# Windowed attention and a gated MLP on one core: value products of 128 and 64 keys, one pool of PSUM banks, and a new order of work

## Chip, cores, metric

The kernel runs on one core of a Trainium2 chip. The metric is the device time of one execution in microseconds, the median of several runs. Five engines work side by side, each through its own instructions in program order, and wait for each other by semaphores: TensorE (PE in the profile; PEld is its weight load), VectorE (DVE), ScalarE (ACT), GpSimd (POOL) and SyncE (SP), which here only issues DMA transfers.

## What is computed

```python
# q, k, v: (8 batches, 8 heads, 576 positions, 64)
scores = q @ k^T / 8                              # within each head
scores = where(0 <= t - s < 128, scores - slope[h] * (t - s), -1e9)
attn = softmax(scores)                            # with + 1e-9 under the sum
x = (attn @ v)  as (8, 576, 512)                  # heads side by side
h = gelu_tanh(x @ w_in)                           # w_in 512 x 1024
u, g = h[..., :512], h[..., 512:]
g = layer_norm(g) * g_ln
g = w_sg @ g + b_sg[:, None]                      # 576 x 576, mixes positions
out = x + (u * g) @ w_out
```

A query looks back at 127 positions and itself, so of each row of scores only 128 keys count.

## The kernel before

The work is cut into 32 pairs of heads (8 batches times 4 pairs) and, per batch, one MLP. Positions are cut into blocks of 64 (R = 64): block 0 comes first by itself, the other eight (numbers 1 to 8) go in four tiles of 128 (T = 4). A query block of 64 sees keys of three blocks, its own and the two before, and 64 of each 192 keys are out of its window in every row. The kernel folds: where a key of the query's own block lies in the future, the score of the key 128 positions earlier takes its place, so each query keeps exactly 128 scores.

A pair passes through these steps, each a letter in the list of work (with the pair's number behind it):

- `q`, `L`: DMA loads of queries and keys (one transfer) and of the values (six: two large ones into `vt`, two small ones, and two of 16 KB into a block-diagonal tile `vd`).
- `*` (or `a` and `c` for the first five pairs): scores, line L247, products of 64 rows by 64 columns, which run on the four quarters of the array.
- `A B C G`: fold (L273) and shift by the bias with a minimum per row (L266), on DVE. `e E f F j`: exponentials on ACT (L282). `R`: inverse of the sums on DVE. `r s S`: scaling on POOL (L299).
- `t T z`: transposes on TensorE (L309, L322). `X Y`: masks (L318), which split each transposed tile into the part that belongs to the own block and the part from 128 earlier, both 128 x 512, each a product of the PSUM tile with a mask (`m_old`, `m_own`). `P`: copy of the first block's weights.
- `2` or `3`: the values of the first block (L329), a product over the block-diagonal `vd`. `v` or `V`: the values of the other blocks (L342). For each head, each 128-key tile is multiplied with the masked weights of up to two query blocks: 6 products of 128 columns and 3 of 64 per head.
- `x`: gather of the two results from PSUM (L350, L351) on ACT. `h l k`: split into a high and a low part for the MLP's products.

The MLP's products run in three terms each (high x high, high x low, low x high, lines L559 to L561). Its steps are `v` (the half that is normalised; for batch 0 it is spread over `w` steps), `u`, `t` (the last 64 positions), then `y` (the mix over positions) and `O` (output). Their evacuations are `vg`, `uc`, `tj`, `gm` (L712) and `oa` (L742). `D` stores. At the start the two weight matrices, which arrive as 8-byte floats, are split into high and low parts: `i` loads, `d` starts on ACT, `m b o` on DVE (L183, L185, L187), `+` on POOL (L190), `H` on ACT, `-` on DVE or POOL (L194). `wl wH w-` do the same for the 4-byte mixing matrix.

The order of all this is one long list, `ORDER`, written out in the kernel. A planner walks it: it holds each step's engine, the steps it comes after and the buffers it takes, asserts that the list respects them, and emits the instructions; each engine then runs its instructions in the list's order. So a step that waits holds up everything behind it on its engine.

PSUM has eight banks of 512 columns. Before, they are three pools with two tiles each: `ps_s` and `ps_a` of one bank for the attention, `ps_m` of two banks for the MLP. One `ps_m` tile holds two steps, for instance `v10` and `v11`, or the two halves `y100` and `y101`, and is given back after the evacuation of both.

Of the kernel before, what the change touches and what calls it, by code (L numbers as in the profile page):

```python
# [21 lines left out]
def attention_gmlp(  # L22
# [30 lines left out]
    TINY64 = 2.0 ** -15  # L53
# [16 lines left out]
    def hi_of(x):  # L70
        return x[:, 0:S]
# [99 lines left out]
    def split64(hi, lo, w, f, last):  # L171
# [9 lines left out]
        nc.scalar.activation(f, w1f, AF.Abs)  # L181
        yield
        nc.vector.tensor_scalar(f, f, TINY64, None, ALU.max)  # L183
# [3 lines left out]
        nc.vector.scalar_tensor_tensor(out=fi, in0=w1, scalar=-0x40000000, in1=fi, op0=ALU.bitwise_and, op1=ALU.bitwise_or)  # L187
# [20 lines left out]
    class Pair:  # L208


        def __init__(self, n):
            self.n, self.b, self.hp = n, n // NPAIR, n % NPAIR
            self.vd, self.p0 = vds[n % 3], p0s[n % 3]
# [9 lines left out]
        def load_v(self):  # L223

            b, c0 = self.b, self.hp * 2 * D
            vt = self.vt = att.tile([P, 2 * T + 1, 2 * D], F32, name="vt", bufs=2)
            cs = slice(c0, c0 + 2 * D)
            for i in range(2):
                nc.sync.dma_start(vt[:, i * T:(i + 1) * T, :], v[b, i * R:i * R + T * P, cs].rearrange("(t p) d -> p t d", p=P))
                nc.sync.dma_start(vt[i * R:(i + 1) * R, 2 * T, :], v[b, 0:R, cs])  # L230
            for j, js in enumerate(self.heads):
                nc.sync.dma_start(self.vd[js, js], v[b, 0:R, c0 + j * D:c0 + (j + 1) * D])

        def scores(self, *t2s):
            insts = [x for t2 in t2s for x in self.score_list(t2, ps_a if len(t2s) > 1 and t2 == 0 else ps_s)]
            burst(insts)

        def score_list(self, t2, pool):
# [5 lines left out]
            banks = self.banks[t2] = [pool.tile([P, 512], F32, name=pool.name) for _ in range(2)]  # L244
# [23 lines left out]
        def minima(self, t2, j):  # L268
# [23 lines left out]
        def inverse(self):  # L292
            rr = self.rr = att.tile([P, NS], F32, name="rr", bufs=3)
# [13 lines left out]
        def transpose(self, j):  # L307
            ct = self.ct[j] = ps_a.tile([P, 512], F32, name="ps_a")
            burst([lambda t=t: nc.tensor.transpose(ct[:, t * P:(t + 1) * P], self.pr[j][:, t, :], ident) for t in range(T)])  # L309

        def masked(self, j):
# [3 lines left out]
            xv = x.rearrange("p (h t b c) -> p t h b c", h=2, t=T, b=2)  # L315
            cv = self.ct.pop(j).rearrange("p (t h c) -> p t h c", t=T, h=2)
            for i, m in enumerate((m_old, m_own)):
                nc.vector.tensor_tensor(xv[:, :, :, i, :], cv, m.rearrange("p (t h c) -> p t h c", t=1, h=1).broadcast_to([P, T, 2, R]), ALU.mult)  # L318
# [557 lines left out]
```

## Time and profile before

| | |
|---|---|
| median of 3 runs | 635.64 us (635.51 to 636.70) |
| the profiled execution | 635.48 us, span 633.8 us |
| busy share of the span | PE 95%, PEld 87%, DVE 59%, ACT 56%, POOL 37% |
| granted TensorE clock, mean | 0.985 of full |
| instructions | 14834, of them 5664 matrix products |
| DMA | 57.24 MB, mean 90 GB/s; 211 to 236 GB/s in the first tenth |
| largest groups on TensorE | the nine groups of the MLP's 288-column products, 2304 products, 75 to 79 us each |

A group's busy time is the sum of its instructions' durations. Products on TensorE are pipelined, so a product of 288 columns that lasts 295 ns is followed by the next 133 ns later; lengths in the chain that ended last tell more of their cost than their durations. Idle time of an engine is put down to what ended it.

### The profile page before, as it was taken

The numbers are of one execution on the slowest core, as the hardware profiler recorded it, in microseconds if no ns is written. First come the engines' busy times: TensorE is split into PE (matmuls) and PEld (weight loads), VectorE is DVE, ScalarE is ACT, GpSimd is POOL, SyncE is SP. The second block draws the span as 40 slices with busy tenths as digits, with TensorE's granted clock in tenths as the row PEclk, the third lists the DMA queues.
The fourth block names the chain that finished last, engine by engine and source line by source line (L and its number), as shares of the span: only waits on it lengthen the run. The fifth ranks groups of instructions, "written<-read, shape, count | busy, mean of one in ns | idle before, by whom it ended". The sixth has DMA issues, their size and how long they took to land.

```text
span 633.8 us, 14834 instructions
## 1 busy us (share of the span) xinstructions
PE 603.6 (95%) x5664; PEld 550.9 (87%) x5664; DVE 374.3 (59%) x1297; ACT 355.4 (56%) x1047; POOL 232.7 (37%) x237
## 2 busy tenths in 40 slices
PE   2687999989999999999999999999999999999997
PEld 1466799978999989998899989998999989999896
DVE  4779897537654786455723577647564565462611
ACT  6687768462673854834672578647473455543430
POOL 2668635542135222542134333542235221441220
PEclk9878999999999999999999999999999999999999
DMA  5777503241203243131220432333122311110001
GB/s 211 223 229 236 158 31 116 79 143 38 73 18 97 95 140 93 42 112 41 78 79 2 134 133 78 86 108 97 40 95 79 128 65 41 41 40 38 0 1 76
DMA packets 55931, 57.24 MB, mean 90 GB/s; under 512 B 8498, under 2 KB 45362, under 8 KB 55860
## 3 DMA queue, kind: packets, MB, share of 16 engines
q1 hardware_dynamic: 55860, 56.28, 28.5%
q8 instruction: 45, 0.74, 0.5%
q14 instruction: 26, 0.21, 0.1%
HBM read 46.83 MB, written 9.44 MB: 89 GB/s over the span
## 4 chain that ended last, share of the span: by engine, by line
PE 85%; DVE 4%; ACT 2%; issue 1%; POOL 0%; POOLq 0%; DVEq 0%
PE ps_m L559 21%; PE ps_m L561 20%; PE ps_m L560 20%; PE ps_s L342 8%; PE ps_a L309 4%; PE ps_a L247 4%; PE ps_s L247 3%; ACT e L282 1%; PE ps_m L707 1%; PE ps_m L706 1%; PE ps_m L643 1%; PE ps_m L645 1%; PE ps_s L329 1%; DVE px L318 1%; DVE e L266 1%
## 5 line engine op out<-in xcount | busy, mean ns | idle before, releaser
L282 ACT ACTIVATE e<-e,stats 128x128 f32<-128x128 f32 (+1 forms) x320 | 121.2, 381 | 39.4 <-DVE stats L266 38.4
L299 POOL TENSOR_TENSOR e<-e,rr 128x512 f32<-128x512 f32 (+1 forms) x96 | 80.1, 854 | 134.6 <-DVE rr L295 99.0
L559 PE MATMUL ps_m<-g,wo 128*128 128x288 f32 x256 | 78.7, 308 | 0.0
L559 PE MATMUL ps_m<-ws,vn 128*128 128x288 f32 x256 | 78.6, 307 | 0.0
L559 PE MATMUL ps_m<-xs,wi 128*128 128x288 f32 x256 | 77.6, 303 | 0.1
L561 PE MATMUL ps_m<-g,wo 128*128 128x288 f32 x256 | 75.8, 296 | 0.0
L561 PE MATMUL ps_m<-xs,wi 128*128 128x288 f32 x256 | 75.6, 295 | 0.0
L560 PE MATMUL ps_m<-ws,vn 128*128 128x288 f32 x256 | 75.6, 295 | 0.0
L561 PE MATMUL ps_m<-ws,vn 128*128 128x288 f32 x256 | 75.5, 295 | 0.0
L560 PE MATMUL ps_m<-xs,wi 128*128 128x288 f32 x256 | 75.5, 295 | 0.0
L560 PE MATMUL ps_m<-g,wo 128*128 128x288 f32 x256 | 74.9, 293 | 0.5 <-POOL g L719 0.5
L584 POOL TENSOR_TENSOR rs<-rs,mhalf 128x1 f32<-128x1 f32 (+1 forms) x40 | 31.4, 786 | 109.5 <-DVE rs L581 103.7
L359 POOL TENSOR_TENSOR xs<-xf,xs 128x576 fp32r<-128x576 f32 x32 | 45.4, 1425 | 62.0 <-ACT xs L356 62.0
L318 DVE TENSOR_TENSOR px<-ps_a,m_old 128x512 f32<-128x512 f32 x64 | 43.9, 686 | 41.1 <-PE ps_a L309 27.3
L719 POOL TENSOR_TENSOR g<-u,g 128x576 fp32r<-128x576 f32 x32 | 45.5, 1424 | 51.0 <-ACT g L716 51.0
L282 ACT ACTIVATION_READ_ACCUMULATOR e<-e,stats 128x1 f32 (+1 forms) x320 | 60.3, 188 | 0.0
L247 PE MATMUL ps_s<-qk 64*64 64x192 f32 (+2 forms) x632 | 42.2, 354 | 14.1 <-DMA qk<-qkT 7.9
L559 PE MATMUL ps_m<-wi,xs 128*128 128x512 f32 x128 | 53.6, 419 | 2.1 <-ACT vg L633 2.1
L712 DVE TENSOR_TENSOR u<-ps_m,u 128x576 f32<-128x576 f32 x32 | 24.1, 755 | 52.0 <-PE ps_m L707 49.8
L742 DVE TENSOR_TENSOR xf<-ps_m,xf 128x576 f32<-128x576 f32 x32 | 24.0, 752 | 49.3 <-PE ps_m L561 49.3
L560 PE MATMUL ps_m<-wi,xs 128*128 128x512 f32 x128 | 51.3, 401 | 0.0
L559 PEld LDWEIGHTS ps_m<-xs,wi 128*128 128x128 f32 x256 | 48.3, 188 | 3.4 <-issue 1.6
(122 smaller groups left out, 1523.4 us busy)
## 6 DMA issues: line engine op xcount, KB each, us to landing
qk<-qkT SPq DMA_DIRECT2D x32, 576.0 KB, 3.9
vt<-v_in SPq DMA_DIRECT2D x64, 256.0 KB, 3.5
outT<-xf SPq DMA_DIRECT2D x32, 288.0 KB, 2.1
wst<-w_in SPq DMA_DIRECT2D x8, 512.0 KB, 6.1
vt<-v_in SPq DMA_DIRECT2D x64, 32.0 KB, 3.1
wst<-w_out SPq DMA_DIRECT2D x4, 512.0 KB, 3.9
wst<-w_sgT SPq DMA_DIRECT2D x4, 288.0 KB, 5.1
vd<-v_in SPq DMA_DIRECT2D x64, 16.0 KB, 2.7
```

The source lines that it names most:

```text
L247: return lambda: nc.tensor.matmul(dst, qk[js, 0, q0:q0 + R], qk[js, 1, k0:k1], start=True, stop=True)
L282: nc.scalar.activation(x, x, AF.Exp, bias=self.nm[0:n, i:i + 1], scale=-1.0, accum_out=self.sm[0:n, i:i + 1])
L299: nc.gpsimd.tensor_tensor(x, x, self.rr[0:n, i:i + m].rearrange("p (m o) -> p m o", o=1).broadcast_to([n, m, c]), ALU.mult)
L309: burst([lambda t=t: nc.tensor.transpose(ct[:, t * P:(t + 1) * P], self.pr[j][:, t, :], ident) for t in range(T)])
L318: nc.vector.tensor_tensor(xv[:, :, :, i, :], cv, m.rearrange("p (t h c) -> p t h c", t=1, h=1).broadcast_to([P, T, 2, R]), ALU.mult)
L342: return lambda: nc.tensor.matmul(x1[heads[j], q0 + lo // 2 * R if t < 0 else q0 + t * R:q0 + (hi + 1) // 2 * R], block, px[j][:, (half * ...
L359: nc.gpsimd.tensor_tensor(lo_of(self.xs), self.xf, hi_of(self.xs).bitcast(F32), ALU.subtract)
L559: nc.tensor.matmul(dst, ah, bh, start=(first and i == 0), stop=False)
L560: nc.tensor.matmul(dst, ah, bl, start=False, stop=False)
L561: nc.tensor.matmul(dst, al, bh, start=False, stop=(last and i == n - 1))
L584: nc.gpsimd.tensor_tensor(x["rs"][0:rows], x["rs"][0:rows], mhalf[0:rows], ALU.pow)
L719: nc.gpsimd.tensor_tensor(st[f"g{f}"][:, 1, :], st["u"][:, f, :], st[f"g{f}"][:, 0, :].bitcast(F32), ALU.subtract)
```

## The change

- **Values.** `L` loads the values into ten slots of 128 keys (`vt[P, 2T + 2, 2D]`): one transfer of 256 KB to the lower 64 partitions, six of 64 KB, so that each query block finds its own keys and the block before it in one slot, with the own block in the upper or the lower half by the parity of the tile. The values step becomes 16 products over 128 keys with 64 columns (a query block against its own and the previous block), 14 over 64 keys (the fold, the block two before), and two over 64 keys for the first block, all in one burst `V`. The block-diagonal `vd` and the steps `2`, `3` are gone. The result lies in two banks, even tiles in one and odd tiles in the other, and `x` gathers it in four copies in place of two.
- **Masks.** `m_own` covers all of it; the second masked part is the tile minus the first part. The score fold (`minima`) mirrors this: the replaced block alternates with the tile's parity.
- **PSUM.** Eight single banks, handed out by the planner: a step takes the bank that is free earliest in the list. `u`, `y` and `O` take one bank per half (`uc`, `gm`, `oa` are done per half, too), `v` one per step.
- **Weights.** The split of the 8-byte floats loses one DVE step (`m`, L183), by a scale in the ACT step.
- **A new list.** It begins `q0 i0 i1 wl2 q1 a0 A0 c0 a1 c1 d0 b0 o0 e0 ...`; before it began `i0 q0 wl2 q1 i1 i7 d0 m0 b0 o0 +0 a0 A0 B0 c0 wl0 d7 d1 wH2 e0 ...`.

The diff, cut to its core:

```diff
-    ps_s = ctx.enter_context(tc.tile_pool(name="ps_s", bufs=2, space=PSUM))
-    ps_a = ctx.enter_context(tc.tile_pool(name="ps_a", bufs=2, space=PSUM))
-    ps_m = ctx.enter_context(tc.tile_pool(name="ps_m", bufs=2, space=PSUM))
+    ps = ctx.enter_context(tc.tile_pool(name="ps", bufs=1, space=PSUM))
+    psum = [ps.tile([P, 512], F32, name=f"bank{i}") for i in range(NB)]
+    def bank():
+        return psum[given.pop(0)]
...
-        nc.scalar.activation(f, w1f, AF.Abs)
+        nc.scalar.activation(f, w1f, AF.Abs, scale=REBASE)
         yield
-        nc.vector.tensor_scalar(f, f, TINY64, None, ALU.max)
+        nc.vector.tensor_scalar(fi, fi, 3, None, ALU.logical_shift_left)
         yield
-        nc.vector.tensor_scalar(fi, fi, 3, 0x3FFFFFFF, ALU.logical_shift_left, ALU.bitwise_and)
-        yield
...
-            for i in range(2):
-                nc.sync.dma_start(vt[:, i * T:(i + 1) * T, :], v[b, i * R:i * R + T * P, cs].rearrange("(t p) d -> p t d", p=P))
-                nc.sync.dma_start(vt[i * R:(i + 1) * R, 2 * T, :], v[b, 0:R, cs])
-            for j, js in enumerate(self.heads):
-                nc.sync.dma_start(self.vd[js, js], v[b, 0:R, c0 + j * D:c0 + (j + 1) * D])
+            nc.sync.dma_start(vt[0:R, 0:2 * T, :], blocks[:, 0:2 * T, :])
+            for slot, k in ((0, 1), (1, 2), (2, 0), (3, 2)):
+                nc.sync.dma_start(vt[R:P, slot:slot + 5:4, :], blocks[:, k:k + 5:4, :])
+            for rs, k in ((slice(0, R), 4), (slice(R, P), 3)):
+                nc.sync.dma_start(vt[rs, 2 * T:2 * T + 2, :], blocks[:, k:k + 5:4, :])
...
-            for i, m in enumerate((m_old, m_own)):
-                nc.vector.tensor_tensor(xv[:, :, :, i, :], cv, m.rearrange(...).broadcast_to([P, T, 2, R]), ALU.mult)
+            nc.vector.tensor_tensor(xv[:, 0], cv, over(m_own, 2), ALU.mult)
+            nc.vector.tensor_tensor(xv[:, 1], cv, xv[:, 0], ALU.subtract)
...
-        def values_first(self, pool):
-            self.x2 = pool.tile([P, 512], F32, name=pool.name)
-            nc.tensor.matmul(self.x2[:, 0:R], self.vd, self.p0, start=True, stop=True)
...
+            x1 = self.x1 = [bank() for _ in range(2)]
+            def dst(q):
+                t, half = divmod(q - 1, 2)
+                c0 = (t // 2 * 2 + half) * R
+                return x1[t % 2][:, c0:c0 + R]
+            def pair(q, j):
+                return lambda: nc.tensor.matmul(dst(q)[heads[j]], vt[:, PAIR_SLOT[q], heads[j]], px[j][:, (q - 1) * R:q * R], start=(q in (1, 3)), stop=False, skip_group_check=True)
+            def old(q, j):
+                rs = slice(0, R) if (q - 1) // 2 % 2 else slice(R, P)
+                return lambda: nc.tensor.matmul(dst(q)[heads[j]], vt[rs, OLD_SLOT[q], heads[j]], px[j][rs, (2 * T + q - 1) * R:(2 * T + q) * R], start=False, stop=False, skip_group_check=True)
+            def first(j):
+                return lambda: nc.tensor.matmul(x1[1 - j][heads[j], 2 * T * R // 2:2 * T * R // 2 + R], vt[heads[j], 2 * j, heads[j]], self.p0[heads[j]], start=False, stop=True, skip_group_check=True)
+            insts = [pair(q, j) for a, b in ((1, 3), (2, 4), (5, 7), (6, 8)) for q in (a, b) for j in range(2)]
+            insts += [old(3, 0), old(2, 0), old(3, 1), old(2, 1), old(4, 0), old(5, 0), old(4, 1), old(5, 1)]
+            insts += [old(7, 0), old(6, 0), old(7, 1), old(6, 1), old(8, 0), first(1), old(8, 1), first(0)]
...
-            nc.scalar.copy(xf[:, R:S].rearrange(...), self.x1.rearrange(...))
-            nc.scalar.copy(xf[:, 0:R], self.x2[:, 0:R])
+            for i, x in enumerate(self.x1):
+                nc.scalar.copy(xf[:, R:S].rearrange("p (a t c) -> p a t c", t=2, c=2 * R)[:, :, i, :], x[:, 0:T * R].rearrange("p (a c) -> p a c", a=2))
+                hs = self.heads[1 - i]
+                nc.scalar.copy(xf[hs, 0:R], x[hs, T * R:T * R + R])
...
+                    if c == "ps":
+                        i = free.index(min(free))
+                        assert free[i] < at[n], n
+                        free[i] = max(at[u] for u in users)
+                        given.append(i)
+                        continue
...
-        put("L", "SP", 2.8, [("2" if n - 3 < FIRST else "3", n - 3)], ...)
+        put("L", "SP", 2.8, [], ...)
...
-                take = [("ps_m", [f"vg{b}{t2}", f"vg{b}{t2 + 1}"])]
+                take = [("ps", [f"vg{b}{t}"])]
...
-                nc.scalar.copy(in2(st["u"][:, f, :]), st[f"pu{f}"][:, :, 0:S2])
+                    nc.scalar.copy(st["u"][:, f, halves[i]], st[f"pu{f}{i}"][:, 0:S2])
...
-                nc.vector.tensor_tensor(in2(o), st[f"po{c}"][:, :, 0:S2], in2(o), ALU.add)
+                    nc.vector.tensor_tensor(o, st[f"po{c}{i}"][:, 0:S2], o, ALU.add)
```

More of the change, by code (lines that the diff above doesn't have):

```diff
@@ L243, in score_list @@
                 self.e0 = e0s[self.n % 2]
-            banks = self.banks[t2] = [pool.tile([P, 512], F32, name=pool.name) for _ in range(2)]
+            banks = self.banks[t2] = [bank() for _ in range(2)]
             def score(dst, js, q0, k0, k1):
@@ L307, in transpose @@
         def transpose(self, j):
-            ct = self.ct[j] = ps_a.tile([P, 512], F32, name="ps_a")
+            ct = self.ct[j] = bank()
             burst([lambda t=t: nc.tensor.transpose(ct[:, t * P:(t + 1) * P], self.pr[j][:, t, :], ident) for t in range(T)])
@@ L399, in run @@
             assert sorted(order) == sorted(self.steps)
+            at = {n: i for i, n in enumerate(order)}
+            free = [-1] * NB
             for n in order:
@@ L407, in run @@
                 yield run
+                assert not given, n
                 done.add(n)
-    BUFS = {"ps_s": 2, "ps_a": 2, "ps_m": 2, "e": 4, "qk": 2, "vt": 2, "nb": 3, "rr": 3, "px": 2, "xf": 2 * NC, "xs": NC, "g": NF, "vg": 2, "vn": 1, "vA": 1, "u": 1, "st": 3}
+    BUFS = {"ps": NB, "e": 4, "qk": 2, "vt": 2, "nb": 3, "rr": 3, "px": 2, "xf": 2 * NC, "xs": NC, "g": NF, "vg": 2, "vn": 1, "vA": 1, "u": 1, "st": 3}
     plan = Planner(BUFS)
@@ L654, in his @@
                 return [st["vA"][0:R], vB[0:R]]
-            add(f"tt{b}", "PE", 1.9, at, sums, [f"k{n}" for n in mine] + rows + [f"{k}{c}" for c in range(NC) for k in "-H"], take=[("ps_m", [f"tj{b}"])])
+            add(f"tt{b}", "PE", 1.9, at, sums, [f"k{n}" for n in mine] + rows + [f"{k}{c}" for c in range(NC) for k in "-H"], take=[("ps", [f"tj{b}"])])
             add(f"tj{b}", "DVE", 1.35, at - AHEAD, join, [f"tt{b}"], take=[("vg", [f"tn{b}"]), ("vg", [f"tj{b}"])])
@@ L794, in attention_gmlp @@
-        l5 l7 r8 O02 *9 oa02 A9 B9 C9 G9 k5 f9 k6 e9 F9 j9 E9 R9 O01 v10 vg10 oa01 v11 s9 vg11 t9 nv01b nv11b X9 q11 L8 D03
-        D00 D02 L9 D01 q10 v12 r9 S9 s8 nv11p S8 nv01p nv01c nv11c u100 T9 Y9 z9 P9 k7 nv01h nv11h vn11 vn10 v13 39 z8 vg12
-        V9 t8 u101 nv21b vg13 P8 T8 tt1 uc10 u110 nv31b nv21c X8 Y8 nv21p nv31p nv21h x9 *10 nv31c nv31h vn12 vn13 u111 tj1
-        A10 B10 tg1 nt1b uc11 C10 nt1c u130 u120 u131 38 G10 nt1p V8 e10 u121 f10 nt1h j10 E10 F10 x8 uc12 uc13 ug1 tn1 *11
@@ L841, in attention_gmlp @@
-        y731 Oa7 gm73 gh73 gl73 O70 O72 oa70 D70 O73 oa72 D72 O71 oa73 D73 oa71 D71
+        q0 i0 i1 wl2 q1 a0 A0 c0 a1 c1 d0 b0 o0 e0 d1 B0 C0 b1 o1 G0 A1 +0 j0 wH2 f0 E0 F0 R0 B1 C1 G1 w-2 +1 s0 r0 S0 t0 z0
+        T0 i4 q2 L0 wl0 wl3 H0 d4 b4 o4 +4 i5 q3 f1 wH0 P0 e1 F1 j1 E1 w-0 -0 d5 wH3 a2 c2 X0 Y0 A2 R1 s1 r1 S1 B2 C2 V0 G2
+        e2 w-3 t1 z1 T1 X1 i6 i3 L2 i2 L1 a3 c3 E2 j2 d6 x0 P1 h0 F2 f2 b5 b6 o5 o6 +5 A3 B3 R2 C3 Y1 l0 s2 +6 S2 r2 G3 w10
+        t2 V1 T2 z2 d3 i7 q4 a4 b3 o3 +3 q5 wl1 H4 H1 f3 e3 k0 j3 F3 E3 x1 h1 H5 H6 P2 d2 d7 -1 R3 X2 Y2 A4 s3 l1 r3 S3 B4
@@ new lines, in attention_gmlp @@
+        e8 e9 F9 E9 l7 O011 O031 O000 R9 R8 v10 v12 vg10 u100 oa001 nv01b oa000 r9 nv01c s8 s9 nv01p uc100 nv01h vg12 nv21b
+        vn10 v11 t9 nv21c nv21p nv21h vg11 nv11b nv11c k5 v13 u110 r8 S9 vn12 k4 S8 O021 k7 u131 vg13 uc131 nv31b oa021 k6
+        O010 z8 P8 oa011 nv31c tt1 z9 oa010 X9 oa031 nv31p nv11p nv11h nv31h T9 Y9 vn11 vn13 u111 u101 L9 P9 V9 L8 D00 tj1
+        q11 L10 q10 D01 tg1 x9 t8 u121 uc121 uc111 uc110 u130 nt1b X8 T8 Y8 O030 oa030 nt1c nt1p uc130 u120 V8 nt1h uc120
+        uc101 x8 ug1 *10 tn1 A10 *11 B10 e10 h8 C10 y131 gm131 G10 y111 gm111 F10 f10 E10 j10 R10 A11 B11 y110 C11 E11 gm110
@@ L842, in attention_gmlp @@
+        D63 D62 D73 D71 D70 D60 D72
     """
```

332 lines of the change are left out of this document (162 added, 170 removed).

## The prediction

> **What bounds the kernel now.** I read the page first, then busy time by stage, then TensorE's waits between the ramp and the end, and then the chain that ended last inside one pair.
>
> ```profile
> span 633.8 us, 14834 instructions
> ```
>
> ```profile
> 0.00:36.00 36.00, 17.39 (x164) 13.18 (x168) 20.19 (x99) 23.52 (x82) 18.26 (x28) 0.89 0.70 227
> 36.00:61.40 25.40, 21.14 (x246) 15.63 (x238) 23.68 (x91) 21.27 (x77) 18.22 (x16) 0.90 0.73 209
> 61.40:79.00 17.60, 17.18 (x141) 13.77 (x141) 14.76 (x44) 13.13 (x39) 11.55 (x12) 0.98 0.58 183
> 79.00:127.00 48.00, 48.00 (x507) 45.52 (x505) 36.75 (x123) 31.01 (x86) 21.71 (x21) 1.00 0.26 78
> 127.00:144.00 17.00, 14.88 (x110) 12.71 (x111) 6.18 (x33) 9.61 (x39) 7.59 (x8) 0.90 0.42 136
> 144.00:618.00 474.00, 473.69 (x4426) 439.20 (x4425) 269.75 (x906) 256.88 (x726) 154.00 (x154) 1.00 0.23 70
> 618.00:633.80 15.80, 11.32 (x84) 10.86 (x82) 3.03 (x4) 0.00 (x0) 1.36 (x1) 0.94 0.20 76
> ```
>
> The columns after the stretch and its length are busy us of PE, PEld, DVE, ACT and POOL, then the granted clock, the DMA share and GB/s. From 61.4 to 618 us TensorE is busy nearly without a break: a microsecond less of its work there is a microsecond less of time. Before 61.4 us nothing is full except DVE in the second part (23.68 of 25.4). Between 79 and 618 us PE's waits have one entry worth naming:
>
> ```profile
> PE ps_m L559 <- ACT vg L633: 2.1, 1, 2.1
> ```
>
> The median of the runs is 635.64 us; the profiled execution took 635.48 us, 1.7 more than its span. I work from 635.5.
>
> **Values, per pair.** These are pieces of the chain inside pair steps at 241 to 246 us, and the forms of the value products.
>
> ```profile
> 241.06 0.17 PE ps_s L329 x2
> 241.23 0.44 PE ps_a L309 x4
> 241.67 1.81 PE ps_s L342 x36
> 246.20 0.65 PE ps_s L247 x14
> ```
>
> ```profile
> L342 PE MATMUL ps_s<-px,vt 128*64 128x128 f32 x648 | 40.0, 273 | 0.0
> L342 PE MATMUL ps_s<-px,vt 128*64 128x64 f32 x324 | 19.9, 229 | 0.0
> ```
>
> The two forms belong to 27 pairs: 24 passes of 128 columns and 12 of 64 each. The code issues 12 and 6 products, so a product is two passes. Four transposes of 128 columns take 0.44, hence 0.110 us per 128-column pass. The second score burst is 8 products, 16 passes of 192 columns, four abreast on the quarters of the array: four slots in 0.65, 0.1625 each. The difference of 64 columns is 0.0525, which puts a 64-column pass at 0.0575. The value burst runs two heads abreast: 12 slots at 0.110 plus 6 at 0.0575 are 1.665, and the remaining 0.145 of its 1.81 is what it costs to change the shape of the array and start. With the separate first values (0.17) a pair pays 1.98.
>
> After: 8 query blocks times 2 heads over all 128 keys, two abreast, 16 slots of 0.0575 = 0.92. Then the folds on quarters: blocks 3, 4, 7, 8 and one first block share a quarter, the other quarters hold 3 or 4, so the longest is 5 products, 10 slots = 0.575. The shape changes twice: 128x64 at the start, 64x64 between. The second change is not in the trace as such. Its bounds are 0 (both shapes halve the columns) and 0.145 (the residue above). I take 0.145, the only change of shape that has a price here. Sum 0.145 + 0.92 + 0.145 + 0.575 = 1.785, a gain of 0.195 per pair; without the change 1.64, a gain of 0.34. Of the 32 pairs the first five do their values in the ramp, where they don't set the end: 27 x 0.195 = **5.3 us**, upper end 9.2.
>
> The Trainium skill, TensorEngine Tiling (Array Packing), Key Properties, says that changing the tiling mode, not just the tile, drains the engine. By that rule the value step is the 1.785 I take; read as no rule for a change of rows alone, it would be 1.64.
>
> Can four 64-column passes start within 0.0575? In the first score burst, four starts fall into this stretch of 0.05 us (PE count):
>
> ```profile
> 245.19:245.24 0.05, 0.04 (x4) 0.04 (x4) 1.00 0.00 0
> ```
>
> So I take slots, not starts, as the bound.
>
> **The wait at 138 us.** This is TensorE's order of time, with ACT's evacuation.
>
> ```profile
> 137.73 0.39 PE L561 MATMUL ps_m<-wi,xs 128*128 128x512 f32 x1
> 140.24 0.58 PE L559 MATMUL ps_m<-wi,xs 128*128 128x512 f32 x1 [2.12 <-ACT vg L633]
> 140.62 0.63 PE L560 MATMUL ps_m<-wi,xs 128*128 128x512 f32 x1
> 143.99 0.39 PE L559 MATMUL ps_m<-wi,xs 128*128 128x512 f32 x1
> 144.22 0.40 PE L560 MATMUL ps_m<-wi,xs 128*128 128x512 f32 x1
> ```
>
> ```profile
> 139.59 0.60 ACT L633 ACTIVATE vg<-ps_m 128x512 f32<-128x512 f32 x1
> ```
>
> `v10` and `v11` write two halves of one `ps_m` tile, and in the list `vg10` reads between them; `v11` waits for that read, which waits on ACT behind two pairs' exponentials. Then nine products from 140.24 to 143.99 need 3.75 us; at the 0.23 seen after it they need 2.1. The wait costs 2.1 + 1.6 = 3.7. With a bank for each `v` step nothing ties `v12` to `vg10`, and the new list has `v10 v12 vg10 u100`: at least 12 products at 0.23 = 2.8 us of free work. What is late next is `vg10` itself, which then only holds a bank. I take the whole **3.7 us**; lower end 0.
>
> **The ramp.** First products, the first exponentials, the first values, and DVE:
>
> ```profile
> 7.31 1.76 PE L247 MATMUL ps_s<-qk 64*64 64x64 f32 x24 [7.31 <-DMA qk<-qkT]
> 29.31 0.66 PE L329 MATMUL ps_a<-p,vd 128*128 128x64 f32 x2 [2.78 <-DMA vd<-v_in]
> ```
>
> ```profile
> 12.11 0.66 ACT L179 ACTIVATE wst<-wst 128x512 int32<-128x512 uint32 x1 [4.72 <-DMA wst<-w_in]
> 14.87 0.39 ACT L282 ACTIVATE e<-e,stats 128x128 f32<-128x128 f32 x1
> ```
>
> ```profile
> L183 DVE TENSOR_SCALAR tmp<-tmp x12: 409/422/520, 7.4 to 91.1; 128x512 f32<-128x512 f32 x12
> ```
>
> ```profile
> 43.78 1.20 DVE px L318 x2
> 57.16 1.21 DVE px L318 x2
> ```
>
> ACT stands 4.72 us before 12.11 for the second weight block while the first scores have long been ready: `d7 d1` stand ahead of `e0`. In the new list `q0` is issued before `i0`, and `e0` follows `d0`, so `e0` can run some 5 us earlier. The first values wait for the `vd` load, issued late on SP behind staging buffers; the new list has `L0` ahead of `wl0 wl3`, and the `vd` load is gone. Between the two DVE rows the chain hardly leaves DVE. L183 goes: 8 of the 12 lie before 61.4 us, four of them after 36 us on that chain, 4 x 0.42 = 1.7. Against it the second mask now reads what the first wrote: two ops that took 1.20 become up to 2 x 0.69, +0.17 per head at most; with six on the chain, 1.0. So the sure part is 0.7. The other end: DVE works 43.9 us up to 61.4 and idles 17.5; some 6 are unavoidable (nothing to do before the first scores) and 11 might be packed. PE, ACT, POOL and the DMA share of 0.7 leave room for that, but each piece also waits for the others. I take **5 us**, about half, with ends -1 (a loss, below) and 11.
>
> **The loads** (first row within 0 to 60 us; second from the page).
>
> ```profile
> vt<-v_in SPq DMA_DIRECT2D x10, 256.0 KB, 5.4
> vd<-v_in SPq DMA_DIRECT2D x64, 16.0 KB, 2.7
> ```
>
> `L` is 7 issues of 640 KB in place of 6 of 608, and 256 KB go to 64 partitions only. It waits no longer for the first values of three pairs back; `q` and `i` queue behind it on SP. Five loads in the ramp at 5% more of 5.4 are 1.4 us on the DMA side, covered by its idle share; if not, that is the loss of 1 above. Later the DMA share is 0.23: nothing.
>
> **Smaller parts.**
>
> ```profile
> L350 ACT COPY xf<-ps_s 128x512 f32<-128x512 f32 x27 | 15.8, 585 | 43.8 <-PE ps_s L342 43.7
> L351 ACT COPY xf<-ps_s 128x64 f32<-128x64 f32 x27 | 5.9, 217 | 0.0
> L689 ACT COPY u<-ps_m 128x576 f32<-128x576 f32 x32 | 20.1, 636 | 30.3 <-PE ps_m L561 30.3
> L742 DVE TENSOR_TENSOR xf<-ps_m,xf 128x576 f32<-128x576 f32 x32 | 24.0, 752 | 49.3 <-PE ps_m L561 49.3
> ```
>
> The gather becomes two copies of 256 columns (0.37 each, on the line through 585 and 217) and two of 64 (0.217): 1.18 for 0.80, 12 us more ACT in all. The `u` copies in halves: 0.40 each by the same line, 5 us more. Gate and output sums in halves: each half between 0.38 and 0.75, I take 0.42, 5 us more DVE. ACT (257 of 474) and DVE (270 of 474) have the room; I cost them at nothing. If that cover fails, it is the last pair before a batch's `v` and `u` steps that is 0.4 late, eight times 0.4 = 3 us. PE's `u`, `y` and output products keep their number. A step now takes one bank and gives it back after its half, and eight banks serve all: no loss visible, gains only where PE waited, which was at 138 us. At the end the last sum is a half:
>
> ```profile
> 629.90 0.76 DVE xf L742
> ```
>
> 0.76 - 0.42 = **0.35**. The list puts `D71 D70 D60` shortly before `D72`; three 288 KB stores are likely through when it starts.
>
> Sum: 635.5 - 5.3 - 3.7 - 5 - 0.35 = **621.1**.
>
> **Rivals.**
> (a) The ramp doesn't shorten beyond its sure 0.7, because DVE stays its bound: 625.4. For it: 23.68 of 25.4. Against: 17.5 us of idle DVE before.
> (b) More is won: no second change of shape (another 3.9) and 11 in the ramp: 611.
> (c) Slower, by the folds. The only measured rate of four-abreast passes is 16 in 0.65, 0.041 each. If that is a cost per pass and not of 192 columns, 32 fold passes take 1.30 and not 0.575, the step 2.51, 0.53 above now, 14.3 us in all: 640.8. It decides once a pass costs more than 0.035 (9.05 / 27 = 0.335 above 1.98). Against: four starts in 0.05 us.
> (d) Slower, by starving. TensorE's order is fixed; if the new one puts a product behind a bank whose reader is late on ACT or DVE, each such place costs about the 3.7 of the wait at 138 us. Four undo the sum; five give 640. Against: one such place in 540 us now, and more banks.
> (e) A floor per start. If a fold pass can only start at twice the spacing of those four starts (2 x 0.05 / 4 = 0.025), the 32 passes take 0.80, the step 2.01, and the time is 635.5 + 0.8 - 9.05 = 627.2. For it: four starts are a short burst, 32 are not. The Trainium skill, TensorE: Matmul & The Clock Gate, Wait — 56ns, not 53.3ns?, states such a floor: start to start never under about 25 ns however few the columns. The trace's four starts in 0.05 us don't agree with it as long as they fall on different quarters.
>
> **Numbers.** My forecast (616 to 625 around 621) 0.50; (a) 0.17; (b) 0.14; (c) 0.05; (d) 0.07; (e) 0.07. For 8 in 10 the range runs from 611.5, just short of (b)'s end, to 630, past (a) and (e). No change within 0.2% (1.3 us, about what a measurement of this kernel can tell) needs (c) or (d) to hit the sum by chance: 0.03. Slower 0.09, faster 0.88.
>
> **What would show it.** The value burst at 1.7 to 1.8 with 64 passes and no L329 beside it; if it is over 2.0, the step on slots is wrong. No PE wait on the `vg` activation near 138 us, and the clock 1.00 from the ramp on; new entries in PE's waits would be (d). First values near 20 us and PE full from about 56 us, not 61.4: if it is still 61, the ramp is wrong. ACT 17 us and DVE 5 to 10 us busier at the same place in the chain (a few per cent).

## The result, and the profile after

| | before | after |
|---|---|---|
| median | 636.07 us (635.51 to 636.70, 4 runs) | 610.43 us (608.44 to 610.87, 4 runs) |
| ratio, 95% interval | | 0.9591 (0.9567 to 0.9614) |
| profiled execution, span | 635.48 us, 633.8 us | 608.44 us, 606.7 us |

The gain is 25.6 us; forecast were 14.4 (621.0), and the range ended at 611.5, 1.1 too early. A second timing of the same kernel gave 608.37 us and 0.9584 (0.956 to 0.9609). From the page of the kernel after:

```profile
span 606.7 us, 16591 instructions
PE 580.5 (96%) x6496; PEld 535.9 (88%) x6496; DVE 377.5 (62%) x1348; ACT 364.9 (60%) x1145; POOL 231.4 (38%) x234
```

The same stretches as before (busy us of PE, PEld, DVE, ACT, POOL; granted clock; DMA share; GB/s):

```profile
0.00:36.00 36.00, 18.30 (x253) 13.61 (x253) 26.77 (x132) 31.31 (x113) 21.44 (x29) 0.84 0.91 248
36.00:61.40 25.40, 22.82 (x335) 18.40 (x332) 22.42 (x77) 23.07 (x84) 19.27 (x18) 0.95 0.81 242
61.40:79.00 17.60, 17.60 (x178) 16.61 (x177) 16.81 (x33) 13.36 (x31) 11.01 (x12) 1.00 0.41 100
127.00:144.00 17.00, 17.00 (x170) 15.71 (x169) 12.09 (x25) 5.97 (x17) 3.16 (x5) 1.00 0.00 1
```

In the first 36 us DVE and ACT are busy 33% longer than before (26.77 for 20.19, 31.31 for 23.52) and the DMA share is 0.91 for 0.70: the ramp is packed more densely. From 127 to 144 us TensorE, which had stood for 2.1 us, is busy throughout. Its last wait before 62 us ends at 48.0 us. Its first scores and first values come 2.6 and 7.7 us earlier than before (7.31 and 29.31):

```profile
4.68 1.58 PE L244 MATMUL bank<-qk 64*64 64x64 f32 x20 [4.68 <-DMA qk<-qkT]
21.58 1.15 PE L340 MATMUL bank<-px,vt 128*64 128x64 f32 x32
```

TensorE's waits behind 62 us are these, all of them (engine, line, releaser; us in total, times, longest):

```profile
PE bank L244 <- DMA qk<-qkT: 2.0, 2, 1.2
PE bank L577 <- POOL g L739: 0.3, 1, 0.3
```

Here is the chain that ended last, inside two pairs (start, length, what). In the first the scores of the next pair (L244) follow the values directly, in the second the MLP does:

```profile
325.04 1.08 PE bank L340 x32
326.13 0.56 PE bank L345 x26
...
326.85 1.48 PE bank L244 x31
328.33 0.33 PE bank L576
328.66 0.13 PE bank L577
```

```profile
508.48 1.58 PE bank L244 x34
510.06 1.08 PE bank L340 x32
511.15 0.56 PE bank L345 x26
...
511.87 0.33 PE bank L576
```

The value step is 511.87 - 510.06 = 1.81; forecast was 1.785. With scores behind it, values and scores together take 328.33 - 325.04 = 3.29, apart 1.81 + 1.58 = 3.39. The step ends in products on 64 x 64 quarters, the shape that scores use, so the array's shape stays. One entry into the MLP's shape is saved too: its first product takes 0.33, the next 0.13. That makes 0.10 + 0.20 = 0.30 us for each such neighbour. The new list has 21 of them, the old one none. The forecast had no term for this. The tail, from the chain:

```profile
603.10 0.46 DVE xf L762
```

It is 0.30 shorter than before (0.76); forecast was 0.35.

### The profile page after: what moved, and what is told of

The parts are those of the page before. It is cut to its first block, busy times and chain, and to the rows that moved or that the text cites. A ratio compares the mean times of both kernels' runs of the same rounds, so it can differ in the third digit from the quotient of the medians.

```text
span 606.7 us, 16591 instructions
## 1 busy us (share of the span) xinstructions
PE 580.5 (96%) x6496; PEld 535.9 (88%) x6496; DVE 377.5 (62%) x1348; ACT 364.9 (60%) x1145; POOL 231.4 (38%) x234
## 4 chain that ended last, share of the span: by engine, by line
PE 88%; DMA 6%; SPq 2%; ACT 1%; POOL 1%; issue 1%; DVE 0%; POOLq 0%
PE bank L576 22%; PE bank L577 21%; PE bank L578 21%; PE bank L244 7%; PE bank L340 5%; PE bank L308 4%; PE bank L345 3%; DMA qk<-qkT 3%; PE bank L725 1%; PE bank L724 1%; DMA vt<-v_in 1%; PE bank L660 1%; PE bank L662 1%; SPq L227 1%; DMA wst<-w_in 1%; POOL g L739 1%
## 5 line engine op out<-in xcount | busy, mean ns | idle before, releaser
L576 PE MATMUL bank<-ws,vn 128*128 128x288 f32 x256 | 78.3, 306 | 0.0
L576 PE MATMUL bank<-g,wo 128*128 128x288 f32 x256 | 77.7, 304 | 0.0
L576 PE MATMUL bank<-xs,wi 128*128 128x288 f32 x256 | 76.8, 300 | 0.0
L577 PE MATMUL bank<-g,wo 128*128 128x288 f32 x256 | 75.7, 296 | 0.3 <-POOL g L739 0.3
L578 PE MATMUL bank<-g,wo 128*128 128x288 f32 x256 | 75.6, 295 | 0.0
L578 PE MATMUL bank<-xs,wi 128*128 128x288 f32 x256 | 75.6, 295 | 0.0
L577 PE MATMUL bank<-xs,wi 128*128 128x288 f32 x256 | 75.6, 295 | 0.0
L577 PE MATMUL bank<-ws,vn 128*128 128x288 f32 x256 | 75.5, 295 | 0.0
L578 PE MATMUL bank<-ws,vn 128*128 128x288 f32 x256 | 75.4, 295 | 0.0
L601 POOL TENSOR_TENSOR rs<-rs,mhalf 128x1 f32<-128x1 f32 (+1 forms) x40 | 29.7, 746 | 112.3 <-DVE rs L598 112.2
L244 PE MATMUL bank<-qk 64*64 64x192 f32 (+2 forms) x1280 | 56.6, 319 | 12.2 <-DMA qk<-qkT 12.2
L263 DVE CUSTOM_DVE_ANT_0 e<-bank,bias 128x128 f32<-128x128 f32 (+1 forms) x256 | 59.2, 269 | 2.3
L244 PEld LDWEIGHTS bank<-qk 64*64 64x64 f32 x1280 | 45.5, 141 | 15.8 <-DMA qk<-qkT 13.4
L316 DVE TENSOR_TENSOR px<-bank,m_own 128x512 f32<-128x512 f32 x64 | 43.7, 682 | 22.2 <-PE bank L308 17.8
L272 DVE COPY_PREDICATED bank<-sel,bank 128x128 f32<-128x128 uint8 x128 | 36.5, 285 | 28.1 <-PE bank L244 28.1
L576 PE MATMUL bank<-wi,xs 128*128 128x512 f32 x128 | 51.8, 404 | 1.6 <-ACT xs L367 1.6
L578 PE MATMUL bank<-wi,xs 128*128 128x512 f32 x128 | 50.9, 397 | 1.8 <-POOL xs L370 1.8
```

Of the source, the lines that this page charges most:

```text
L244: return lambda: nc.tensor.matmul(dst, qk[js, 0, q0:q0 + R], qk[js, 1, k0:k1], start=True, stop=True)
L263: nc.vector.tensor_tensor_reduce(out=dst, in0=src, in1=bs, scale=-1.0 / math.sqrt(D), scalar=3e38, op0=ALU.add, op1=ALU.min, accum_out=acc)
L272: nc.vector.copy_predicated(bank[:, 2 * R:4 * R].rearrange("p (i c) -> p i c", i=2), sel.rearrange("p (i c) -> p i c", i=2), ends)
L316: nc.vector.tensor_tensor(xv[:, 0], cv, over(m_own, 2), ALU.mult)
L576: nc.tensor.matmul(dst, ah, bh, start=(first and i == 0), stop=False)
L577: nc.tensor.matmul(dst, ah, bl, start=False, stop=False)
```

## The experiments

Differences in us are (ratio to the kernel before, timed on the same chip, minus that of the kernel compared with) x 635.5; a ratio carries an interval of about 0.0024 to either side (1.5 us), a difference of two some 2 us.

| kernel | median us | ratio (95%) |
|---|---|---|
| changed kernel, timed again | 608.37 | 0.9584 (0.956 to 0.9609) |
| changed, old list | 625.12 | 0.9847 (0.9822 to 0.9871) |
| new list for 39 steps, then old | 620.86 | 0.9777 (0.9753 to 0.9802) |
| new list for 161 steps, then old | 620.30 | 0.9773 (0.9751 to 0.9795) |
| new list for 416 steps, then old | 613.51 | 0.9669 (0.9642 to 0.9696) |
| old list to 80 us, then new | 624.19 | 0.9841 (0.9815 to 0.9867) |

**The list and the code apart.** The list of before can be taken over step by step into the changed kernel, and cut at any place where buffers allow.

```diff
-    ORDER = q0 i0 i1 wl2 q1 a0 A0 c0 a1 c1 d0 b0 o0 e0 ...
+    ORDER = i0 q0 wl2 q1 i1 i7 d0 b0 o0 +0 a0 A0 B0 c0 ...   (a_oldlist; a_newramp from *9 on; a_oldramp up to *9)
```

> The changed kernel again, unaltered, beside the three others of this call, as the common point that their lists are compared with. 610 to 611.

> The changed kernel with the order of before (its list taken over step by step, the steps that are gone left out, halves side by side): values, loads, masks, banks and split as after, only the order is the old one. Theory (the prediction's code terms are right and what it missed lies in the list): the code is worth 5.3 for the values, 3.7 to 4 for the wait, about 2.6 for the split and 0.35 for the tail, so 635.5 less 12 gives about 623 to 624, and the list 13. Rival 1 (the ramp is shorter by the code, with the loads and the values in one burst, whatever the order): 616 to 618. Rival 2 (the new list is needed for the banks to pay): above 626.

> The changed kernel with the new list up to the first scores of pair 9 (about 80 us) and the old order behind it, in which no value step is followed by scores (21 are in the new list). Theory: the ramp of the new list is worth 7 to 8 on top of the code, the neighbourhood of values and scores and the fewer entries to the MLP's shape 4 to 6: 615 to 616.5. Rival (the neighbourhood is worth nothing, all is the ramp): within 1.5 of 610.4.

> The changed kernel with the old order up to the first scores of pair 9 and the new list behind it. Theory: 7 to 8 us more than the new kernel, about 618; TensorE's work at 80 us is as far behind as in the kernel with the old list throughout. Rival (what the old ramp loses is made up later, or the ramp hangs on the code): under 3 us more.

The code alone is worth 9.7 us (1 - 0.9847), the new order up to pair 9 11.3 more (7 to 8 expected), the rest of the new order 5.4. My code terms were 5.3 + 3.7 + 0.35 = 9.35, close to the 9.7, but partly by luck: the shorter split is in the 9.7 and not in the 9.35, and in the kernel before it is worth 2 to 4 us by itself (below). So under the old list the new code loses about as much somewhere, and no run separates it. With the old list the changed code leaves the ramp as it was; TensorE does not get ahead (first row up to 36 us, and so on):

```profile
0.00:36.00 36.00, 15.80 (x219) 12.31 (x223) 20.46 (x100) 24.95 (x86) 17.80 (x25) 0.76 0.74 214
36.00:61.40 25.40, 19.40 (x272) 14.08 (x264) 21.33 (x76) 20.41 (x79) 16.15 (x16) 0.87 0.84 218
61.40:79.00 17.60, 15.69 (x191) 12.57 (x190) 15.42 (x48) 14.40 (x45) 13.26 (x13) 1.00 0.67 201
```

The same with the new list for the first 80 us:

```profile
0.00:36.00 36.00, 19.39 (x271) 14.34 (x273) 27.94 (x134) 32.26 (x119) 22.46 (x30) 0.85 0.87 253
36.00:61.40 25.40, 23.55 (x327) 19.12 (x324) 22.44 (x78) 23.24 (x80) 19.27 (x18) 0.95 0.83 246
61.40:79.00 17.60, 17.60 (x179) 16.45 (x179) 16.94 (x34) 13.35 (x31) 10.56 (x12) 1.00 0.33 84
```

TensorE's recorded products up to 79 us are 777 in the second and 682 in the first, and in the second from 61.4 us on it no longer stands. With the old list ACT waits for weight blocks, in the changed kernel it hardly does (waits up to 62 us, old list first):

```profile
ACT wst L178 <- DMA wst<-w_in: 9.7, 4, 4.3
```

```profile
ACT wst L178 <- DMA wst<-w_in: 1.5, 3, 0.9
```

The old ramp with the new list behind it was to cost 7 to 8 and costs 0.9841 - 0.9584, 16.3: the ramp's 11.3 and nearly all of the 5.4. Behind 62 us its TensorE waits 6.0 us in all, 3.5 of them for queries, against 1.9 in the changed kernel (timed again); with the old order there, the kernel with the old ramp (`a_oldlist`) waits 2.2 and the one with the new ramp (`a_newramp`) 0.6. So waits account for (6.0 - 1.9) - (2.2 - 0.6) = 2.5 of the 5.0 us between 16.3 and 11.3. The rest I have not resolved.

**Where in the ramp.** The new list for 39 steps (to the first transposes), for 161 (to about 40 us), and the latter with two loads moved:

```diff
-    ... h2 j4 i10 c4 T3 C4 f4 G4 F4 tl L3 L4 ...
+    ... h2 j4 tl L3 i10 c4 T3 C4 f4 G4 F4 L4 ...   (a_new161b)
```

> The changed kernel with the old order, but for the first 39 steps of the new list (up to the transposes of pair 0). Theory 1 (the head decides: q0 issued first, e0 right after the first split step): 3 to 5 of the 11.6 us are here, 620 to 622. Theory 2 (the order of the weight and value loads behind the head decides; with the old list ACT stands 9.7 us before 62 us for weight blocks, with the new one 1.5): within 1.5 of the 625.1 of the old list.

> The changed kernel with the new order up to the scores c of pair 4 (161 steps, about 40 us) and the old order behind. Theory 2 (the loads): 8 to 12 of the 11.6 us are there by then, 613.5 to 617. Rival (the ramp is won between 40 and 80 us, where the old order leaves TensorE idle): 621 or more.

> The kernel with 161 steps of the new order, and the loads tl and L3 ahead of i10 as in the new list, the rest old. Theory (in the ramp TensorE's start is set by loads that stand in SP's queue behind a wait for a staging buffer): SP's gap from 40.5 to 48 us closes, L3 is issued near 41 us and not 49, and 3 to 7 us go: 613.5 to 617. Rival (the order of ACT, DVE and PE in this stretch is what counts): within 1 us of 620.3.

The head brings 0.9847 - 0.9777, 4.4 us (theory 1). A part of that can come by way of the granted clock: the mean of each execution is 0.994 to 0.997 with the new head and 0.981 to 0.985 with the old list. The next 122 steps bring nothing (0.9773), the last 255 the remaining 6.6. For these I blamed SP's queue. That fell: with tl and L3 ahead the DMA share from 36 to 61.4 us goes from 0.60 to 0.85, as it should, and the time stays (0.977). Rows of the 161-step kernel, first without, then with the two moved:

```profile
36.00:61.40 25.40, 21.68 (x308) 16.47 (x307) 19.33 (x74) 18.02 (x67) 17.51 (x16) 0.78 0.60 185
```

```profile
36.00:61.40 25.40, 20.36 (x249) 15.18 (x251) 18.49 (x68) 18.24 (x70) 17.62 (x17) 0.79 0.85 246
```

What stays is this, in the order of time of ACT and of TensorE in the 161-step kernel:

```profile
49.23 1.15 ACT L189 ACTIVATE wi<-tmp 128x512 fp32r<-128x512 f32 x2 [3.81 <-POOL tmp L187]
50.29 0.35 ACT L360 COPY xf<-bank 128x256 f32<-128x256 f32 x1
```

```profile
50.91 2.05 PE L244 MATMUL bank<-qk 64*64 64x192 f32 x16 [3.08 <-ACT xf L362]
```

ACT stands 3.81 us at a weight step that waits for POOL; the gather of pair 2 is queued behind it; and TensorE stands 3.08 for the bank that this gather gives back. It is a wait on a bank with a late reader, as in rival (d), at a place where two orders meet. With tl and L3 moved it is still there (3.2 us). The new list has the gather `x2` ahead of these weight steps (`H2`, `H7`). That this order explains the 6.6 us is argued; no run moved it alone.

**Parts of the change, put into the kernel before.**

```diff
-        i0 q0 ... c0 wl0 d7 d1 wH2 e0 E0 j0 ...
+        q0 i0 ... c0 wl0 e0 E0 j0 d7 d1 wH2 ...                     (b_head)
-        ... O01 v10 vg10 oa01 v11 ...
+        ... O01 v10 oa01 v11 vg10 ...                               (b_vg)
-        nc.scalar.activation(f, w1f, AF.Abs)
+        nc.scalar.activation(f, w1f, AF.Abs, scale=REBASE)          (b_split, to the end)
         yield
-        nc.vector.tensor_scalar(f, f, TINY64, None, ALU.max)
-        yield
-        nc.vector.tensor_scalar(fi, fi, 3, 0x3FFFFFFF, ALU.logical_shift_left, ALU.bitwise_and)
+        nc.vector.tensor_scalar(fi, fi, 3, None, ALU.logical_shift_left)
...
```

> The kernel before, with its list changed at the head alone: q0 is issued ahead of i0, and e0 E0 j0 stand ahead of d7 d1 wH2. Theory (the ramp is set by the order in which the first pair gets its inputs and its ACT time): the first scores move from 7.3 to about 4.7 us, the first exponential from 14.9 to about 8 to 10 us, and TensorE's work is ahead by 3 to 5 us at 79 us, so about 631 to 633. Rival (the ramp is bound by the loads and by DVE, whoever comes first): the first exponential comes earlier, but the time stays within 1 us of 636, since later steps wait for the weights that were put behind.

> The kernel before, with vg10 one step later in the list, behind v11; both halves of the shared tile are then written before it is read. Theory (the wait at 138 us is the tie of v11 to vg10 alone): the 2.1 us wait and the slow clock behind it go, 3.7 us less, about 632.4. Rival (another step waits there for the same late work on ACT): a wait of about the same length stands at the next MLP step, and the time stays within 0.7 us of 636.

> The kernel before, with the shorter split of the 8-byte weights (one DVE step fewer per block, 12 in all, of 0.42 us). Theory of the prediction (only the four that lie on DVE's chain between 36 and 61.4 us count): 1.7 us less, about 634.4. Rival 1 (DVE waits for the loads): within 0.5 us of 636. Rival 2 (DVE bounds all of the ramp): 8 x 0.42 = 3.4 us less, about 632.7.

> The three edits together: head of the list, vg10 behind v11, shorter split. Theory: they add up, 3.7 for the wait and 3 to 7 for the ramp, 625 to 629; what is then left to 610.4 is the work of the value steps and of the new list. Rival (the ramp does not move without the new loads and the rest of the new list): only the wait goes, about 632.

| | median us | ratio (95%) | us |
|---|---|---|---|
| b_head | 636.50 | 1.0023 (1.0004 to 1.0042) | +1.5 |
| b_vg | 629.37 | 0.9915 (0.9894 to 0.9936) | -5.4 |
| b_split | 631.15 | 0.9935 (0.9915 to 0.9955) | -4.1 |
| b_all3 | 630.34 | 0.9915 (0.9893 to 0.9938) | -5.4 |

The tie at 138 us is shown: with `vg10` one step later TensorE's wait is gone, and so is the slow clock behind it.

```profile
127.00:144.00 17.00, 17.00 (x131) 14.85 (x130) 9.65 (x40) 7.92 (x33) 7.79 (x10) 1.00 0.35 107
```

I expected 3.7 and measured 5.4 (4.1 to 6.7). The traces split this. The values of pairs 7 and 9 start at 125.12 and 153.23 us before and at 122.89 and 147.07 in `b_vg`: between them 3.9 us are gone, the wait and its slow clock, and the 2.2 us before them lie in the ramp, where the list is the same and the granted clock is not (last section).

The shorter split measures 4.1 (2.9 to 5.4), more than the 1.7 I expected. Here, too, a part can be the ramp's clock: among executions of like mean clock, 631.2 to 633.3 us before (0.996) stand beside 630.3 and 630.8 (0.997), some 2 us. Whether four blocks count or all eight (3.4) stays open. The head moves the first scores from 7.31 to 4.67 and the first exponential from 14.87 to 11.08:

```profile
4.67 1.76 PE L247 MATMUL ps_s<-qk 64*64 64x64 f32 x24 [4.67 <-DMA qk<-qkT]
```

```profile
11.08 0.40 ACT L282 ACTIVATE e<-e,stats 128x128 f32<-128x128 f32 x1 [2.22 <-DVE stats L266]
```

but the time does not follow: an earlier start of the first pair is lost again in the ramp. The three together give 5.4, where 8.0 would be their sum. The difference of 2.6 is no larger than the uncertainty of the four ratios together, and the ramp's clock enters each of them, so whether they add up stays open. In the changed kernel the new head (39 steps, more than is moved here) is worth 4.4, here less than nothing.

**Parts taken out of the kernel after.** A DVE step is put back (`a_m`), and the neighbours of values and scores are separated in 19 places (`a_sep`; there are 21, not 22).

```diff
+        nc.vector.tensor_scalar(f, f, 0.0, None, ALU.max)     (a_m)
-   V13 *15 A15 ... y201          (a_sep, in 19 places)
+   V13 y201 *15 A15 ...
```

> The changed kernel, with one more DVE step of 128 x 512 in the split of each block of 8-byte weights (a max with 0, which changes nothing), as long as the one that was taken out, 0.42 us. Theory (in the new order the ramp is set by the loads and SP, with DVE at 13.6 of 36 us and 18.4 of 25.4 less full than before): under 1 us more. Rival (DVE is still on the chain): 8 x 0.42 = 3.4 us more, about 613.8.

> The changed kernel, with one MLP step put between the value step and the next pair's scores in 19 of the 22 places where the scores follow the values directly. Theory (values that end in products of 64 x 64 and scores that begin with them need no change of the array's shape): the value steps in front go from 1.71 to 1.80, the scores from 1.48 to 1.58, and about as many more entries into the MLP's shape come in, each 0.05 to 0.1; 3 to 5 us more, 613.5 to 615.5. Rival (the change of shape costs nothing, the steps are only attributed otherwise): within 0.6 us of 610.4.

The theory for `a_m` took DVE's busy time from the wrong column: 13.6 and 18.4 are PEld's, and DVE is busy 26.77 of 36 and 22.42 of 25.4 us (result section).

`a_m`: 612.05 us, 0.964 (0.9613 to 0.9667), 3.6 us more than the changed kernel, near the rival: DVE is on the chain of the new ramp too. In its trace the first values of pair 5 start at 82.95 us, against 80.37 in the changed kernel (timed again) and 79.98 (the first time): 2.6 to 3.0 us are lost by then. Behind the ramp it differs at the two waits for queries; one of them, at 246 us, has the clock at half behind it and costs its profiled execution 3 us more.

`a_sep`: 619.29 us, 0.9754 (0.973 to 0.9778), 10.8 us more, twice what I expected. Nineteen neighbours at 0.30 are 5.7. The price can be read from the traces directly. In seven stretches between two value steps, a moved MLP step is the only difference in TensorE's order, and TensorE waits in neither kernel; each is longer in `a_sep`, by 0.28 to 0.35 us. One of them, pairs 24 to 25, in the changed kernel (timed again) and in `a_sep`, lasts 7.06 and 7.37 us:

```profile
431.88 1.15 PE L340 MATMUL bank<-px,vt 128*64 128x64 f32 x32
438.94 1.15 PE L340 MATMUL bank<-px,vt 128*64 128x64 f32 x32
```

```profile
440.55 1.15 PE L340 MATMUL bank<-px,vt 128*64 128x64 f32 x32
447.92 1.15 PE L340 MATMUL bank<-px,vt 128*64 128x64 f32 x32
```

TensorE's waits behind 79 us in `a_sep`, all of them, say where some more went:

```profile
PE bank L577 <- POOL g L739: 2.4, 5, 0.8
PE bank L576 <- DVE stats L263: 0.9, 2, 0.6
PE bank L340 <- DVE px L317: 0.3, 1, 0.3
```

These are 3.6 us, as moved MLP steps come too early for their operands; the changed kernel has 1.9, nearly all for queries. So 5.7 + 1.7 of the 10.8 are accounted for, and some 3 us stay unexplained. The list's later part, 5.4 us for 20 more neighbours (6.0 by the rows), agrees with the price.

**The shapes of the values.**

```diff
-                rs = slice(0, R) if (q - 1) // 2 % 2 else slice(R, P)
+                rs = slice(0, P)                                            (a_fold128, a_fold128b)
-            insts += [old(3, 0), old(2, 0), old(3, 1), ... old(8, 0), first(1), old(8, 1), first(0)]
+            insts += [old(q, j) for q in (3, 2, 4, 5, 7, 6, 8) for j in range(2)] + [first(1), first(0)]   (a_fold128b)
-            insts = [pair(q, j) ...] + [old(q, j) ...] + [first(j) ...]
+            insts = [one 128x128 product] + [wide(k, j) ...] + [narrow(k, j) ...]                           (a_oldval)
```

> The changed kernel, with the folds as products over 128 rows (the other half of the weights is zero) and not on quarters of the array. Theory of the prediction (slots of 0.0575 us; quarters run four abreast): the 14 folds take 7 x 2 slots on two halves, 0.805 for 0.575, and the first block's values are a shape of their own, 0.115 and one more change, 0.145: the step goes from 1.80 to about 2.1, 8 to 9 us more over 27 pairs, about 619. With the loss of the same shape ahead of the scores it could be 621. Rival (four abreast brings no more than two abreast, passes are bound by their starts): the step stays near 1.8 to 1.9, at most 3 us more.

> The changed kernel with the folds over 128 rows, heads in turn, so that neighbours lie in different halves of the array's columns. Slots of 0.0575: 14 for the folds 0.805, 2 for the first block 0.115, one more change of shape 0.145, against 0.575 now: the step 2.1, 8 to 10 us more in 27 pairs, 617 to 620. Rival (two abreast do not overlap in this part, whatever the order): as with two of one head in a row, a step of 2.57 and about 632.

> The changed kernel, with the value step in the old shapes: one product of 128 rows, 12 of 128 columns and 6 of 64 columns, to the same two banks. Its values are not the right sums; only its time is looked at. Theory: the step costs 1.98 as before (1.81 and 0.17 for the first block), 0.2 more than the new one, and the scores behind it have to change the shape again: 5.3 us for the shapes and 2 to 4 for the neighbours, 617 to 620. Rival (the gain of the new step is in the fewer weights per product or the loads, not in the shapes): within 2 us of 610.4.

`a_fold128`: 633.08 us, 0.9965 (0.9944 to 0.9985), 24 us more; `a_fold128b`: 619.42, 0.9766 (0.9739 to 0.9792), 11.6 more, with 8 to 10 expected. One value step of each from the chain, `a_fold128` first:

```profile
333.18 0.81 PE bank L345 x26
333.99 0.25 PE bank L349 x2
334.25 0.26 PE bank L345 x2
334.51 0.25 PE bank L349 x2
```

```profile
518.60 1.08 PE bank L340 x32
519.68 0.82 PE bank L345 x28
520.50 0.26 PE bank L349 x4
520.76 0.33 PE bank L575
```

I had blamed the order of the heads for the 24 us. It isn't that: 26 fold passes take 0.81 with two of one head in a row, 28 take 0.82 in turn. It is the first block's two products (L349, two passes each, 64 rows) that stand between folds of 128 rows: each change of shape shows as 0.25 for two passes of 0.0575, 0.135 to 0.145 a change. That is the price I had taken for a change of shape from a residue. Quarters against halves: 26 passes in 0.56 in the kernel after, 28 in 0.82 here.

`a_oldval`: 618.45 us, 0.974 (0.9716 to 0.9764), 9.9 more. A step with scores behind it, from the chain:

```profile
323.90 0.17 PE bank L345 x2
324.07 1.46 PE bank L340 x24
325.53 0.35 PE bank L343 x12
325.88 1.58 PE bank L244 x34
```

The step is 0.17 + 1.46 + 0.35 = 1.98, as expected, and the scores behind it take 1.58, where they take 1.48 behind the new step. 27 x 0.17 + 21 x 0.10 = 6.7 of the 9.9. In its trace the values of pair 5 start 2.7 us later than in the changed kernel (timed again), so most of the rest lies in the ramp, where I have not resolved it. The loads are those of the changed kernel, so the shapes carry the gain of the value step: 4.6 us, where I had 5.3.

**Toward a better version.** Queries loaded ahead of values and stores on SP (`a_loads`), and with that scores of three more pairs moved behind values (`a_imp`).

```diff
-   L10 q10 ... D03 D02 q12 q13 ... D12 L15 q16
+   q10 L10 ... q12 q13 ... D03 D02 ... q16 D12 L15
```

> The changed kernel with the loads q10, q12 and q13 and q16 ahead of the value loads and stores that they wait behind on SP, and the scores of pairs 8, 9 and 31 moved behind the values in front of them (24 such neighbours, not 21). Theory: the waits for queries near 152 and 241 us go, 1.6 us, and each new neighbour is worth 0.27: 606.0. Rival (the wait moves to the next step, as TensorE waits for the same load chain): within 0.6 of 608.4.

> The changed kernel with q10, q12, q13 and q16 moved ahead of value loads and stores on SP, and nothing else. Theory: the two waits for queries near 152 and 241 us go, and the time is 1.6 us less, 606.8 beside 608.4. Rival (TensorE then waits at the same place for the folds or the values): no change, within 0.6.

`a_imp` gives 0.9607 (0.9574 to 0.964), 1.5 us more than the changed kernel with an uncertainty of some 2.6. The 2.4 us less that I expected do not show, and why is open. `a_loads` gives 607.65 us (605.53 to 610.89), 0.9581 (0.9555 to 0.9606). In its trace both waits for queries are gone; this is all that TensorE waits for between 80 and 600 us:

```profile
PE bank L577 <- POOL g L739: 0.3, 1, 0.3
```

From the values of pair 5 to those of pair 15 it takes 168.2 us, and the changed kernel (timed again) 170.2. So the trace bears out the theory with 2.0 us; the timing, 0.2 us with an uncertainty of 2, can't tell. It is the fastest median, not a shown gain.

## Why the prediction was wrong

- **Values: right.** The step takes 1.81 us for the 1.785 forecast. The slots held (32 passes of 128 rows in 1.08, where I had 0.145 + 0.92 = 1.065), and so did the second change of shape, 0.145, which the trace of before did not show: `a_fold128` has it at 0.135 to 0.145. The Trainium skill, TensorEngine Tiling (Array Packing), Key Properties, has the rule (a change of mode drains the engine); the trace agrees, also for a change of rows alone. Rivals (c) and (e) fall: 26 fold passes in 0.56 are 0.0215 a pass, with the change of shape in it. The Trainium skill, TensorE: Matmul & The Clock Gate, Wait — 56ns, not 53.3ns?, states that start to start never drops below about 25 ns; across quarters the trace doesn't agree, over a burst of 26 now and not only of four.
- **The wait at 138 us: right.** `b_vg` shows it at 3.9 us in its trace for the 3.7 forecast; no new wait took its place there.
- **The ramp: the step that failed.** "I take 5 us, about half, with ends -1 ... and 11." The new order's ramp measured 11.3, the upper end. Halving the idle time of DVE was no estimate of a schedule. Three pieces are known: the head 4.4, nothing to about 40 us, 6.6 from there to pair 9; what makes the last one is argued. My sign for it, TensorE full from about 56 us, came at 48. "4 x 0.42 = 1.7" for the shorter split is probably too small as well: 4.1 taken out before and 3.6 put back after by the medians, 2 to 3 where the traces and the clock allow a closer look.
- **What the forecast lacked: the new list's later part, 5.4 us.** I read the list for waits, and not for which step stands next to which. `V` ends in the scores' shape, and 21 times scores now follow: 0.30 each by the rows, and 0.28 to 0.35 where `a_sep` takes a neighbour apart. I priced the change of shape inside the step and did not look at the one behind it.
- **The range.** Its lower end came from (b), 11 in the ramp and a missing change of shape. The ramp's 11 came without the latter; 635.5 less 9.35 for the code and 11.3 is 614.9, inside. The neighbours carried it out: 609.5, beside 610.43 measured.
- **Loads and smaller parts.** "Later the DMA share is 0.23: nothing" held but for two waits for queries behind value loads on SP, 2.0 us. ACT became 9.5 us busier and DVE 3.2, where I had 17 and 5 to 10; behind 62 us no wait of TensorE names them, as said.

## What to carry to other kernels

Count the changes of the array's shape over the whole order of work and not inside a step: let a step end in the shape that the next one begins with. A ramp in which several queues are nearly full is a schedule: a step that starts earlier need not bring the end forward, as the head moved alone showed. To price a new order, run the new code with the old one, then cut the orders at a few places. To price one kind of step, compare two traces between steps that both have, where nothing else was moved; a time of the whole adds waits and the ramp's clock to it. An experiment that changes an operation should keep the shapes of its neighbours, or it measures them.

## What was new about the hardware

The granted clock in the ramp differs from one execution to the next with the same work. The stretch from 30 to 36 us, in the kernel before and in `b_vg`, whose list is the same up to 138 us:

```profile
30.00:36.00 6.00, 5.22 (x49) 4.66 (x53) 3.24 (x19) 3.27 (x12) 5.26 (x5) 0.50 0.90 297
```

```profile
30.00:36.00 6.00, 4.87 (x58) 4.22 (x57) 3.88 (x20) 3.33 (x13) 5.26 (x5) 1.00 0.91 299
```

In the runs of the kernel before that go with these, a mean clock of 0.996 stands beside 631.2 to 633.3 us and 0.985 beside 635.3 to 635.6: some 2 us, which a comparison of single executions would take for a gain. At the values of pair 7, up to which the lists are the same, `b_vg`'s trace is ahead by 2.2 us. The Trainium skill, TensorE: Matmul & The Clock Gate, What's actually happening, gives a reason that fits: the window in which activity is counted runs freely, so the phase differs from run to run. The rows agree in that the same list got 0.50 once and 1.00 once.
